# Transposing two row tiles ahead of the first modulation columns, with filler matmuls between the small steps, in a fused adaLN, linear attention and SwiGLU block

## The chip, the cores and the metric

The kernel runs on one core of one Trainium2 chip. The metric is its time in device microseconds; the span of a profile is about 2 us shorter than the time of the same execution. All times are medians, with the lowest and the highest run. There is a second number for each run, the mean clock granted to TensorE, where 1.000 is full speed; 3.4 us at half speed shows as 0.998. It counts only what the clock record lists. The record starts at 5.48 us in the profile before, and the fillers ahead of that already ran at half speed (0.43 us from start to start, 0.22 us after it). This first slow stretch is in every profile (its end, seen from the fillers, lies at 5.5 to 8.4 us) and in no mean clock; "half clock" and "full clock" below are meant after it.

## The reference

The block normalises x, scales and shifts it by columns that come from a vector c (the "modulation"), applies linear attention, and then does the same with a SwiGLU feed-forward. The change touches only the start of the first half.

```python
def reference(A_x, A_wqkv, A_wo, B_x, B_w_gate, B_w_up, B_w_down, c, w_mod):
    x = A_x                                        # 1 x 2048 x 1024, bf16
    mod = (silu(c) @ w_mod).reshape(...)           # w_mod: 1024 x 6144
    sa, ca, ga, sb, cb, gb = ...                   # six rows of 1024
    h = layernorm(x) * (1 + ca) + sa               # "wsa" holds sa's weights, "wca" ca's
    x = x + ga * linear_attention(h, A_wqkv, A_wo)
    h = layernorm(x) * (1 + cb) + sb
    return x + gb * swiglu(h, B_w_gate, B_w_up, B_w_down)
```

## The kernel before

The first q matmul needs three things: normalised and transposed rows of x, the first modulation columns, and the first q weights. All of it is loaded by one queue, in this order, and no load up to the last one shown waits for a compute engine. One part of wca, wsa or wq is 512 KB.

```python
        P.dma("c", CS8[0:NDT, :], cv8)
        for st in range(4):
            P.dma("x0_%d" % st, XRES[:, st, :], xv[:, st, :])
        # ... cut: ca_load, wq_load, sa_load issue one part each ...
        for p in range(4):
            ca_load(p)
            sa_load(p)
            if p < 3:
                wq_load(p)
        for i in range(6, 8):
            P.dma("wq%d" % i, ...)
        # then four row tiles of x for chunk 1, then the k weights
```

A filler is a matmul of a zero tile with the identity, into a bank that is overwritten before anybody reads it. It only keeps TensorE busy.

```python
        def warm(n=1, bank=2):
            for _ in range(n):
                P.pe("matmul", out=PS[:, bank, :], lhsT=IDENT[:], rhs=E1[:, 0, :], start=True, stop=True)
```

The modulation columns are products with one moving column, and 16 of them make the two columns of one pair. `fin_ca` is the small column arithmetic on VectorE; `h0_first` and `h0_scale` scale and shift the transposed rows with the columns.

```python
        def mod_pair(p):
            mod_sc(WCA, 8, range(2 * p, 2 * p + 2))
            mod_sc(WSA, 0, range(2 * p, 2 * p + 2))
            for f in fin_ca(p):
                f()
            for dt in range(2 * p, 2 * p + 2):
                h0_scale(dt)
```

The q phase of the first chunk takes the weights in parts as they land. (`mod_pair` is written out here; the kernel puts its first two lines into a helper.)

```python
            for nt in range(5):
                q_part(nt, qb[nt], (0, 1), 0, 256)      # first half of the rows
            tile_transposes(2)
            tile_transposes(3)
            # ... cut: scaling and copies of the second half ...
            for nt in range(5):
                if nt == 3:
                    mod_pair(1)
                q_part(nt, qb[nt], (0, 1), 256, 512)
            # ... cut: nt 5 and 6 ...
            for nt in range(7):
                if nt == 4:
                    mod_pair(2)
                q_part(nt, qb[nt], (2, 3))
            for nt in range(7):
                if nt == 4:
                    mod_pair(3)                         # needs the last wca and wsa parts
                q_part(nt, qb[nt], (4, 5))
            # ... cut: dt 6 and 7, and the eighth group; then k, and all the rest
```

Of the kernel before, what the change touches and what calls it, by code (L numbers as in the profile page):

```python
# [264 lines left out]
def bass_adaLN_cond__linear_attn_block__swiglu_ffn__prompt_kernel(  # L265
# [22 lines left out]
    with ExitStack() as es:  # L288
# [6 lines left out]
        def T(name, off, shape, dt):  # L295
            n = 1
            for s_ in shape[1:]:
                n *= s_
            assert off % 32 == 0 and off + n * mybir.dt.size(dt) <= ARENA, (name, off, shape)
            return nc.alloc_sbuf_tensor_at(name, shape, dt, offset=base + off)  # L300
# [4 lines left out]
        WCA = T("wca", 32 * KB, [128, NDT, D], BF16)  # L305
# [134 lines left out]
# [3 lines that stand above are left out]
# [23 lines left out]
        def ln1_xn(st):  # L466
            P.dve("tensor_scalar", out=XRES[:, st, :], in0=XRES[:, st, :],
                  scalar1=MV[:, st, 0:1], scalar2=RSTD[:, st:st + 1], op0=ALU.subtract, op1=ALU.mult)
# [22 lines left out]
        def mod_sc(w, c0, ms):  # L491
            for m in ms:
                for kt in range(NDT):
                    P.pe("matmul", out=PS[:, 0, c0 + m:c0 + m + 1], lhsT=w[:, kt, m * 128:(m + 1) * 128],
                         rhs=SILUC[:, kt:kt + 1], start=mod_first[0], stop=(kt == NDT - 1), skip_group_check=True)
                    mod_first[0] = False

        def fin_ca(p):
            sl, sp = slice(2 * p, 2 * p + 2), slice(8 + 2 * p, 10 + 2 * p)
            return [  # L500
                lambda: P.dve("tensor_copy", out=MODTMP[:, sp], in_=PS[:, 0, sp]),
                lambda: P.dve("tensor_copy", out=MODTMP[:, sl], in_=PS[:, 0, sl]),
                lambda: P.dve("tensor_scalar", out=MODTMP[:, sp], in0=MODTMP[:, sp], scalar1=1.0, scalar2=None,
                              op0=ALU.add),
                lambda: P.dve("tensor_copy", out=MODCOL[:, 1, sl], in_=MODTMP[:, sl]),
                lambda: P.dve("tensor_copy", out=MODCOL[:, 0, sl], in_=MODTMP[:, sp]),
            ]
# [12 lines left out]
        def t_view(dt, n=1):  # L520
            return PSB[:, 6 + dt // 4, (dt % 4) * 256:(dt % 4 + n) * 256]

        def h0_first(dt, half, eng):
            dst = HT[:, 0, dt, 256 * half:256 * half + 256]
            if eng == "act":
                P.act("activation", out=dst, in_=t_view(dt), func=ACT.Identity, scale=MODCOL[:, 0, dt:dt + 1],
                      bias=MODCOL[:, 1, dt:dt + 1])
            else:
                P.dve("tensor_scalar", out=dst, in0=t_view(dt), scalar1=MODCOL[:, 0, dt:dt + 1],
                      scalar2=MODCOL[:, 1, dt:dt + 1], op0=ALU.mult, op1=ALU.add)  # L530

        def raw_copy(dt, n, half, eng):
            dst = HT[:, 1, dt:dt + n, 256 * half:256 * half + 256]
            src = t_view(dt, n).rearrange("p (d q) -> p d q", q=256)
            if eng == "act":
                P.act("activation", out=dst, in_=src, func=ACT.Copy)
            else:
                P.dve("tensor_copy", out=dst, in_=src)
# [5 lines left out]
        def ln1_rstd1(st):  # L544
            P.dve("tensor_scalar", out=VE[:, st:st + 1], in0=MV[:, st, 1:2], scalar1=EPS, scalar2=None, op0=ALU.add)
            P.pool("tensor_tensor", out=RSTD[:, st:st + 1], in0=VE[:, st:st + 1], in1=NEGHALF[:, 0:1], op=ALU.pow)
# [19 lines left out]
        def act_mv_ops(st):  # L566
            return [
                lambda: P.dve("tensor_copy", out=MV[:, st, 0:1], in_=SUMX[:, st:st + 1]),
                lambda: P.dve("scalar_tensor_tensor", out=MV[:, st, 1:2], in0=SUMX[:, st:st + 1],
                              scalar=SUMX[:, st:st + 1], in1=SUMSQ[:, st:st + 1], op0=ALU.mult, op1=ALU.subtract),  # L570
            ]

        def neg_rstd(st):
            P.dve("tensor_scalar", out=VE[:, st:st + 1], in0=MV[:, st, 1:2], scalar1=-1.0, scalar2=EPS, op0=ALU.mult,
                  op1=ALU.add)
            P.pool("tensor_tensor", out=RSTD[:, st:st + 1], in0=VE[:, st:st + 1], in1=NEGHALF[:, 0:1], op=ALU.pow)

        def mixed_mv_ops(st):
            return [
                lambda: P.dve("bn_aggr", out=MV[:, st, :], in_=STATS[:, (st // 4) % 2, st % 4, 0:1, :]),  # L580
                lambda: P.dve("scalar_tensor_tensor", out=MSQ2[:, st:st + 1], in0=MV[:, st, 0:1], scalar=MV[:, st, 0:1],
                              in1=MV[:, st, 1:2], op0=ALU.mult, op1=ALU.add),
                lambda: P.dve("scalar_tensor_tensor", out=MV[:, st, 0:1], in0=MV[:, st, 0:1], scalar=0.5,
                              in1=SUMX[:, st:st + 1], op0=ALU.mult, op1=ALU.add),
                lambda: P.dve("scalar_tensor_tensor", out=SUMSQ[:, st:st + 1], in0=MSQ2[:, st:st + 1], scalar=0.5,
                              in1=SUMSQ[:, st:st + 1], op0=ALU.mult, op1=ALU.add),
                lambda: P.dve("scalar_tensor_tensor", out=MV[:, st, 1:2], in0=MV[:, st, 0:1], scalar=MV[:, st, 0:1],
                              in1=SUMSQ[:, st:st + 1], op0=ALU.mult, op1=ALU.subtract),
            ]
# [4 lines left out]
        m2, m3 = act_mv_ops(2), mixed_mv_ops(3)  # L594

        def tile_transposes(j):
            for dt in range(NDT):
                c = (dt % 4) * 256 + (j % 2) * 128
                P.pe("transpose", out=PSB[:, 6 + dt // 4, c:c + 128], in_=XRES[:, j, dt * 128:(dt + 1) * 128],
                     identity=IDENT[:])  # L600

        warm(11, bank=3)
        mod_sc(WCA, 8, range(2))
        warm(3, bank=3)
        fa = fin_ca(0)
        s0_[0]()
        s0_[1]()
        s1_[0]()
# [2 lines left out]
        s1_[1]()  # L611
        ln1_xn(0)
        tile_transposes(0)
        s1_[2]()
        ln1_rstd1(1)
        s3_[0]()
        m2[1]()
        m2[0]()
        m3[0]()
        neg_rstd(2)  # L620
        fa[0]()
        ln1_xn(1)
        fa[2]()
        m3[1]()
        fa[4]()
        m3[2]()
        mod_sc(WSA, 0, range(2))
        tile_transposes(1)
        m3[3]()
        m3[4]()  # L630
        fa[1]()
        neg_rstd(3)
        fa[3]()
        h0_first(0, 0, "dve")
        h0_first(1, 0, "dve")
        raw_copy(4, 4, 0, "act")
        raw_copy(2, 2, 0, "dve")
        ln1_xn(2)
        ln1_xn(3)

        phi_ctr = [0]
# [521 lines left out]
```

## Time and profile before

| | before |
|---|---|
| time, median of 3 runs | 840.45 us (840.42 to 840.97) |
| span of the profiled run | 838.5 us |
| TensorE busy | 98% of the span |
| first q matmul starts | 13.59 us |
| last shift columns (wsa, pair 3) start | 26.52 us |
| half clock, after the first rise at 5.48 us | 8.89 to 15.72 us |

Three lines of the page of the kernel before: the span, busy time by engine with its share, and the chain of waits by engine.

```profile
span 838.5 us, 10210 instructions
...
PE 825.3 (98%) x4154; PEld 384.1 (46%) x4233; DVE 298.3 (36%) x641; ACT 203.8 (24%) x355; POOL 41.0 (5%) x52
...
PE 95%; SPq 2%; DMA 1%; DVE 1%; issue 1%; ACT 0%; DVEq 0%
...
```

A busy TensorE says nothing of what starts it. The chain of waits of the kernel before, cut to the head, has start, length, and what ran or was waited for (SPq is the sync engine's queue, that is, the issuing of a load):

```profile
17.38 0.47 SPq L178
...
17.89 8.58 DMA wsa<-in_w_mod_dram
26.48 0.04 issue
26.52 2.84 PE ps L178 x26
...
```

Up to 26.48 us the chain is loads and the issuing of loads. From 26.52 us on it is nearly all TensorE. So the span is the start of the last shift columns plus what follows; here 838.5 - 26.52 = 812.0 us. This "rest" is used throughout.

TensorE in the head, in order of time: start, length, operation, tiles, shapes, count, and in brackets the idle time before it and what ended that. "e_92,ident" are fillers, "ident,xres" transposes, "siluc,wca" and "siluc,wsa" modulation columns, "ht,wqk" q matmuls.

```profile
2.76 3.87 PE L178 MATMUL ps<-e_92,ident 128*128 128x512 bf16 x11 [0.37 <-DVE e_92 L178]
9.38 0.59 PE L178 MATMUL ps<-siluc,wca 128*128 128x1 bf16 x16 [2.75 <-DMA wca<-in_w_mod_dram]
...
11.06 1.06 PE L178 MATMUL ps<-ident,xres 128*128 128x128 bf16 x8
...
12.39 1.01 PE L178 MATMUL ps<-ident,xres 128*128 128x128 bf16 x8
13.59 2.29 PE L178 MATMUL ps<-ht,wqk 128*128 128x256 bf16 x10 [0.19 <-DVE ht L178]
...
22.30 0.54 PE L178 MATMUL ps<-siluc,wsa 128*128 128x1 bf16 x16
...
26.52 0.55 PE L178 MATMUL ps<-siluc,wsa 128*128 128x1 bf16 x16 [0.18 <-DMA wsa<-in_w_mod_dram]
...
```

The fillers end at 6.63 us, and TensorE idles 2.75 us until the first wca part has landed. Then everything follows in a row, the two transposes among it. TensorE waited only 0.18 us for the last wsa part.

Stages of the kernel before: the stretch and its length, busy time by engine (PE is TensorE, PEld its weight loads, DVE VectorE, ACT ScalarE, POOL GpSimd; x counts instructions), then the granted clock, the DMA engines' share and their rate.

```profile
core 0: us, PE busy (x) PEld busy (x) DVE busy (x) ACT busy (x) POOL busy (x), PEclk, DMA share, GB/s
...
6.00:10.00 4.00, 1.25 (x20) 0.66 (x19) 2.62 (x11) 3.50 (x7) 1.67 (x3) 0.86 1.10 316
10.00:14.00 4.00, 3.81 (x37) 2.61 (x36) 2.63 (x14) 0.81 (x3) 0.55 (x1) 0.50 1.15 318
...
22.00:26.00 4.00, 3.88 (x54) 2.18 (x54) 1.31 (x7) 0.00 (x0) 0.00 (x0) 1.00 1.12 307
...
```

From 6 us on the DMA engines' share is above 1, at 307 to 318 GB/s in these lines. (The Trainium skill, page "DMA: Bandwidth & Descriptors", section "Specifications", gives about 358 GB/s as the HBM limit for a core; these three lines are 11 to 14% below that.) The clock column shows the half clock.

### The profile page before, as it was taken

To read this page: it belongs to the slowest core of one execution; us is meant where nothing else is said; L and a number is where in the kernel's file an instruction comes from. 1 tells how busy PE (TensorE), PEld (TensorE's weight loads), DVE (VectorE), ACT (ScalarE), POOL (GpSimd) and SP (SyncE) were. 2 spreads that over 40 slices of the span, in tenths; PEclk is the share of its full clock that TensorE was granted. 3 is DMA by queue.
4 is the path that set the end of the run, shared out by engine and by line. 5 is a ranking of instruction groups with operands and counts; after the bars stand their busy time and mean duration, and the time that the engine had idled before them with its cause. 6 is when DMAs were issued, how large, how long until landed. Compare 5 with 4: busy or idle time off the path is not lost.

```text
span 838.5 us, 10210 instructions
## 1 busy us (share of the span) xinstructions
PE 825.3 (98%) x4154; PEld 384.1 (46%) x4233; DVE 298.3 (36%) x641; ACT 203.8 (24%) x355; POOL 41.0 (5%) x52
## 2 busy tenths in 40 slices
PE   7999999999999999999999999999999999999998
PEld 4444444454444444444444444444444444444444
DVE  5777966556974212111221111022121102111111
ACT  4667763213333111100111111021111101111111
POOL 1000000000050000030000003000000300000000
PEclk8999999999999999999999999999999999999999
DMA  9993323747195895540355562045556104553000
GB/s 276 265 323 48 68 89 126 172 136 265 37 248 184 266 296 155 153 80 26 108 153 153 151 157 58 24 114 151 151 150 181 46 13 113 151 152 99 1 25 26
DMA packets 178125, 112.99 MB, mean 135 GB/s; under 512 B 32664, under 2 KB 161824, under 8 KB 178080
## 3 DMA queue, kind: packets, MB, share of 16 engines
q1 hardware_dynamic: 178080, 112.35, 48.1%
q8 instruction: 33, 0.54, 0.3%
q14 instruction: 12, 0.10, 0.0%
HBM read 100.67 MB, written 4.33 MB: 125 GB/s over the span
## 4 chain that ended last, share of the span: by engine, by line
PE 95%; SPq 2%; DMA 1%; DVE 1%; issue 1%; ACT 0%; DVEq 0%
PE ps L178 95%; SPq L178 2%; DMA wsa<-in_w_mod_dram 1%; DVE acc L178 0%; DVE xres L178 0%; DVE mhl L178 0%; ACT mw L178 0%; DVE ve_72 L178 0%; DVE ut L178 0%; DVE mean_70 L178 0%; DVE msq_71 L178 0%; DVE sumx L178 0%; DVEq L249 0%
## 5 line engine op out<-in xcount | busy, mean ns | idle before, releaser
L178 DVE TENSOR_TENSOR at<-sg,ps 128x512 bf16<-128x512 bf16 x112 | 77.0, 688 | 296.1 <-PE ps L178 285.1
L178 ACT ACTIVATE sg<-ps 128x512 bf16<-128x512 f32 x112 | 66.9, 597 | 310.3 <-PE ps L178 298.9
L178 PE MATMUL ps<-wd_a,at 128*128 128x512 bf16 (+2 forms) x519 | 112.8, 372 | 0.5
L178 PE MATMUL ps<-wd_b,at 128*128 128x512 bf16 (+2 forms) x388 | 85.4, 372 | 0.5
L178 PEld LDWEIGHTS ps<-wd_a,at 128*128 128x128 bf16 x528 | 51.1, 98 | 59.8
L178 DVE TENSOR_TENSOR ut<-att,gb_b 128x512 bf16<-128x512 bf16 (+1 forms) x32 | 13.5, 421 | 167.7 <-ACT att L178 167.7
L178 ACT ACTIVATE att<-ps 128x512 bf16<-128x512 f32 (+1 forms) x32 | 17.4, 591 | 182.1 <-PE ps L178 182.1
L178 PE MATMUL ps<-ht,wqk 128*128 128x512 bf16 (+1 forms) x258 | 58.4, 376 | 1.0 <-DVE ht L178 0.5
L178 PEld LDWEIGHTS ps<-wd_b,at 128*128 128x128 bf16 x396 | 38.3, 98 | 44.7
L178 PE MATMUL ps<-wqk,ht 128*128 128x512 bf16 x250 | 56.6, 379 | 0.4
L178 PE MATMUL ps<-mw,pqt 128*128 128x512 bf16 x250 | 55.8, 379 | 0.4
L178 PE MATMUL ps<-h2t,guu_117 128*128 128x512 bf16 x221 | 52.8, 379 | 0.2
L178 PE MATMUL ps<-h2t,guu_115 128*128 128x512 bf16 x219 | 52.6, 379 | 0.3
L178 PE MATMUL ps<-h2t,gug_114 128*128 128x512 bf16 x220 | 52.6, 379 | 0.2
L178 PE MATMUL ps<-h2t,guu_116 128*128 128x512 bf16 x221 | 52.6, 379 | 0.2
L178 PE MATMUL ps<-h2t,gug_111 128*128 128x512 bf16 x220 | 52.5, 379 | 0.2
L178 PE MATMUL ps<-h2t,gug_112 128*128 128x512 bf16 x219 | 52.5, 379 | 0.2
L178 PE MATMUL ps<-h2t,gug_113 128*128 128x512 bf16 x219 | 52.3, 379 | 0.3
L178 PE MATMUL ps<-h2t,guu_118 128*128 128x512 bf16 x217 | 52.1, 379 | 0.3
L178 POOL TENSOR_SCALAR h2t<-h2t,modcol 128x512 bf16<-128x512 bf16 x32 | 28.3, 898 | 394.4 <-DMA h2t<-xn_119 394.4
L178 ACT ACTIVATE e_92<-ps 128x512 bf16<-128x512 f32 x64 | 39.1, 611 | 30.8 <-PE ps L178 27.0
L178 ACT ACTIVATE rl<-ps 128x512 bf16<-128x512 f32 x64 | 38.9, 608 | 0.0
(120 smaller groups left out, 685.5 us busy)
## 6 DMA issues: line engine op xcount, KB each, us to landing
gug_111<-in_B_w_gate_dram SPq DMA_DIRECT2D x14, 512.0 KB, 4.0
guu_115<-in_B_w_up_dram SPq DMA_DIRECT2D x14, 512.0 KB, 5.3
gug_112<-in_B_w_gate_dram SPq DMA_DIRECT2D x14, 512.0 KB, 4.0
guu_116<-in_B_w_up_dram SPq DMA_DIRECT2D x14, 512.0 KB, 5.3
gug_113<-in_B_w_gate_dram SPq DMA_DIRECT2D x14, 512.0 KB, 4.0
guu_117<-in_B_w_up_dram SPq DMA_DIRECT2D x14, 512.0 KB, 5.3
gug_114<-in_B_w_gate_dram SPq DMA_DIRECT2D x14, 512.0 KB, 4.1
guu_118<-in_B_w_up_dram SPq DMA_DIRECT2D x14, 512.0 KB, 5.3
```

The source lines that it names most:

```text
L178: return getattr(e, method)(**kw)
```

## The change

Its intent is to take the wait for the first wca part out of TensorE's path: the transposes of tiles 0 and 1 need no modulation, so they can fill it; tile 1 is normalised earlier for that. The fillers are there to keep the clock at full speed. 14 fillers are removed and 22 added. In the diff, `ln1_xn(j)` normalises row tile j, the `s_`, `m2`, `m3` and `neg_rstd` calls are steps of the rows' statistics, `fa` those of `fin_ca(0)`, and `raw_copy` saves transposed rows for a later pair:

```diff
-        warm(11, bank=3)
-        mod_sc(WCA, 8, range(2))
-        warm(3, bank=3)
         fa = fin_ca(0)
+        warm(13, bank=3)
         # ... cut: statistics and normalisation of tile 0 ...
         tile_transposes(0)
+        warm(2, bank=3)
         s1_[2]()
         ln1_rstd1(1)
         s3_[0]()
+        ln1_xn(1)
+        tile_transposes(1)
+        warm(0, bank=3)
+        mod_sc(WCA, 8, range(2))
+        warm(4, bank=3)
         # ... cut: m2, m3[0], neg_rstd(2) ...
+        m3[1]()
+        m3[2]()
         fa[0]()
-        ln1_xn(1)
+        ln1_xn(2)
         fa[2]()
-        m3[1]()
+        m3[3]()
         fa[4]()
-        m3[2]()
+        m3[4]()
         mod_sc(WSA, 0, range(2))
-        tile_transposes(1)
-        m3[3]()
-        m3[4]()
+        warm(3, bank=3)
+        neg_rstd(3)
         fa[1]()
-        neg_rstd(3)
+        raw_copy(4, 4, 0, "act")
         fa[3]()
         h0_first(0, 0, "dve")
         h0_first(1, 0, "dve")
-        raw_copy(4, 4, 0, "act")
         raw_copy(2, 2, 0, "dve")
-        ln1_xn(2)
         ln1_xn(3)
```

## The prediction

> **What bounds the kernel now.** The page gives TensorE 98% of an 838.5 us span. The change touches only the first 14 us: does a gain there reach the end? In the chain of waits, nothing of the first 26.5 us is TensorE: it is the sync engine issuing loads ([...]2.97 us for the first 512 KB of q weights), then 8.58 us of the last shift-modulation load (wsa part 3). From 26.52 on it is nearly all TensorE, back to back. The stage table shows the DMA engines saturated (share about 1.0 or more, about 320 GB/s) from 4 to 33 us.
>
> Landings, from each issue's start plus its time to landing: wca part 0 9.4, wsa 0 11.0, wq 0 12.5, wca 1 14.3, wsa 1 16.0, wq 1 17.5, wca 2 19.8, wsa 2 21.5, wq 2 23.1, wca 3 24.9, wsa 3 26.5 us. None waits for a compute engine.
>
> **What TensorE does in the head.** Fillers end at 6.6; it idles 2.75 us until wca 0 lands. The granted clock falls to 0.50 at 8.9 and returns at 15.7. The Trainium skill ("TensorE: Matmul & The Clock Gate", Part 1) says free-running windows of 3413 ns set the clock; the trace agrees: the stretches last 3.41 us (full) and 6.83 us (half). Row tile 0, normalised at 7.5, is transposed only at 10.6, tile 1 at 12.4; the first q matmul starts at 13.6.
>
> **What the change does.** Removes 11+3 fillers, adds 13+2+4+3 (net +8, an estimated 0.22 us each at full clock, 1.7 us, in gaps). Both tiles' transposes (1.0 us each at half clock, about 0.5 at full) move ahead of the modulation columns; tile 1's normalisation (0.55 us on VectorE) moves from 10.1 to about 8.5. Estimates: fillers to 7.1, tile 0 transposed 7.6 to 8.1, tile 1 9.1 to 9.6, wca columns to 10.1, fillers to 11.0, wsa columns to 11.6, column arithmetic and scaling of h on VectorE, first q matmul 12.5 to 12.8 (wq 0 lands 12.5). The clock stays full through 16 us, or drops for one window.
>
> **What of it is on the critical path.** TensorE comes to the second half-tile q work 1 to 2 us earlier, but then meets loads: wsa 1 (16.0), wsa 2 (21.5; before it used them at 22.3, so at most 0.8 us is left), wsa 3 (26.5; before it used them at 26.52 after waiting 0.18 us). There nothing is left; the saved time turns into waits for loads. Load order and later stages are unchanged.
>
> **Time.** 840.4 us, range 839.7 to 841.1. Faster by over 2% would need 16.8 us.
>
> **What would show it.** First q matmul at 12.5 to 12.8 (not 13.6). No half clock between 9 and 16 us, or one window. TensorE's waits for wca and wsa loads between 14 and 27 us growing from 0.2 to 1 to 2.5 us. Wsa 3 columns still at 26.5 us, within 0.3; first k matmul (33.1) unmoved; the chain of waits still with loads to 26.5.
>
> **What would make it wrong.** Loads landing earlier because the engines compete less with them (a gain to about 1 us). New idling before wsa 2 and wsa 3 falling badly into a clock window and halving the clock around 27 us (a loss of about 3 us). Fillers or the new VectorE order delaying the first q matmul by more than 1 to 2 us of slack.

## The result, and the profile after

The changed kernel took 839.93 us (839.89 to 841.08, 4 runs), the kernel before 840.43 us (840.24 to 840.97, 4 runs). The ratio is 0.9996, with a 95% interval of 0.9979 to 1.0014: the same. Ratios are the mean time of one kernel's fast runs over that of the other's of the same rounds, so not quite the ratio of the medians quoted.

The same lines of the changed kernel's page:

```profile
span 837.9 us, 10302 instructions
...
PE 829.9 (99%) x4241; PEld 383.6 (46%) x4241; DVE 299.7 (36%) x641; ACT 203.8 (24%) x355; POOL 40.9 (5%) x52
...
PE 96%; SPq 2%; DMA 1%; DVE 1%; issue 0%; ACT 0%; DVEq 0%
...
```

The PE counts must not be compared: 87 more matmuls are listed where the change adds 8 fillers (the weight loads, PEld, differ by just 8), so 79 matmul records are missing in the trace before.

TensorE in the head of the changed kernel (columns as before):

```profile
2.76 4.75 PE L178 MATMUL ps<-e_92,ident 128*128 128x512 bf16 x13 [0.36 <-DVE e_92 L178]
7.68 0.62 PE L178 MATMUL ps<-ident,xres 128*128 128x128 bf16 x8 [0.17 <-DVE xres L178]
...
9.21 0.62 PE L178 MATMUL ps<-ident,xres 128*128 128x128 bf16 x8 [0.47 <-DVE xres L178]
9.66 0.54 PE L178 MATMUL ps<-siluc,wca 128*128 128x1 bf16 x16
...
12.46 1.39 PE L178 MATMUL ps<-ht,wqk 128*128 128x256 bf16 x10 [0.33 <-DVE ht L178]
...
20.83 0.55 PE L178 MATMUL ps<-siluc,wsa 128*128 128x1 bf16 x16 [0.42 <-DMA wsa<-in_w_mod_dram]
...
25.85 0.55 PE L178 MATMUL ps<-siluc,wsa 128*128 128x1 bf16 x16 [0.96 <-DMA wsa<-in_w_mod_dram]
...
```

Both transposes now precede the wca columns, the 2.75 us wait is gone, and the first q matmul starts at 12.46 us, 1.13 us earlier. But then TensorE waits 0.42 us for wsa part 2 and 0.96 us for wsa part 3, where before it waited 0.18 us in all. Its gain has become two waits.

The chain of waits of the changed kernel:

```profile
17.15 8.65 DMA wsa<-in_w_mod_dram
25.80 0.05 issue
25.85 34.26 PE ps L178 x214
```

It has the same shape. The rest is 837.9 - 25.85 = 812.05 us, against 811.98 us before. So all of the 0.6 us by which this span is shorter is that one load landed at 25.80 us, not at 26.48 us. Whether the change caused that is a question for the experiments.

Stages of the changed kernel:

```profile
6.00:10.00 4.00, 3.36 (x38) 1.80 (x37) 3.46 (x15) 3.84 (x9) 1.58 (x3) 1.00 1.14 323
10.00:14.00 4.00, 3.67 (x48) 2.35 (x45) 3.02 (x13) 0.89 (x1) 0.65 (x2) 1.00 1.16 310
...
22.00:26.00 4.00, 3.04 (x34) 1.50 (x32) 0.74 (x2) 0.00 (x0) 0.00 (x0) 1.00 1.14 329
...
```

The clock is full in all these stages (in the first from 6.39 us on), and the DMA rate is the same within a few per cent.

### The profile page after: what moved, and what is told of

Read it like the earlier page. It is cut to its first block, busy times and chain, and to the rows that moved or that the text cites. A ratio compares the mean times of both kernels' runs of the same rounds, so it can differ in the third digit from the quotient of the medians.

```text
span 837.9 us, 10302 instructions
## 1 busy us (share of the span) xinstructions
PE 829.9 (99%) x4241; PEld 383.6 (46%) x4241; DVE 299.7 (36%) x641; ACT 203.8 (24%) x355; POOL 40.9 (5%) x52
## 4 chain that ended last, share of the span: by engine, by line
PE 96%; SPq 2%; DMA 1%; DVE 1%; issue 0%; ACT 0%; DVEq 0%
PE ps L178 96%; SPq L178 2%; DMA wsa<-in_w_mod_dram 1%; DVE acc L178 0%; DVE xres L178 0%; DVE mhl L178 0%; ACT mw L178 0%; DVE ve_72 L178 0%; DVE ut L178 0%; DVE mean_70 L178 0%; DVE msq_71 L178 0%; DVE sumx L178 0%; DVEq L249 0%
```

## The experiments

Theory A: the loads set the head; what the change saves on TensorE turns into waits for the later modulation loads, and the rest, 812.0 us, is untouched. Rival B: TensorE's own work and clock bound the head, and the 0.5 us between the medians is the change's gain. Rival C: the change saves nothing that would last even without those loads. Every run is marked as correct, e7 and e8 too, where the results are wrong, so for these two the mark says nothing. Each was timed in five rounds, beside the kernel before; an interval is about 1 us to either side, so a difference below that is read from the profiles.

A summary of one profiled execution of each, in us. "Last columns" is the start of the last shift columns, and the rest is the span minus that.

| run | time (lowest to highest) | before, same rounds | first q | last columns | rest |
|---|---|---|---|---|---|
| before, first profile | 840.43 (840.24 to 840.97) | - | 13.59 | 26.52 | 811.98 |
| changed, first profile | 839.93 (839.89 to 841.08) | 840.43 | 12.46 | 25.85 | 812.05 |
| r_before | 840.51 (840.05 to 840.73) | 840.47 | 12.68 | 26.59 | 812.01 |
| r_after | 840.72 (839.87 to 841.07) | 840.47 | 12.59 | 26.69 | 812.01 |
| e1_order_only | 840.59 (840.01 to 840.82) | 840.47 | 12.21 | 26.20 | 812.00 |
| e2_fill_only | 840.21 (840.05 to 840.46) | 840.47 | 13.54 | 26.19 | 812.01 |
| e3_delay4 | 840.57 (840.20 to 842.22) | 840.52 | 12.47 | 26.09 | 812.01 |
| e4_delay14 | 842.73 (841.62 to 844.40) | 840.52 | 12.31 | 28.71 | 811.99 |
| e5_extra_load | 842.82 (842.01 to 845.46) | 840.52 | 12.87 | 28.51 | 814.89 |
| e6_q7_early | 840.39 (839.76 to 842.51) | 840.52 | 12.27 | 27.05 | 811.25 |
| e7_light_before | 839.05 (837.63 to 840.04) | 840.75 | 12.86 | 24.98 | 812.02 |
| e8_light_after | 838.09 (837.95 to 838.39) | 840.75 | 12.30 | 23.94 | 811.96 |
| e9_q7_mid | 840.27 (839.98 to 840.52) | 840.75 | 12.62 | 26.11 | 811.89 |
| e10_load_fill | 842.39 (841.97 to 844.12) | 840.65 | 12.36 | 30.04 | 812.06 |

### r_before and r_after: both kernels again

No edit.

> The kernel before, again, as a control. Both theories: ratio 1.000 within 0.1%. Its use is the spread of the landing of the last shift-modulation load (26.5 us in the first profile) and of the clock record in the head: if the landing moves by some 0.5 us from execution to execution of one program, the 0.68 us by which it was earlier in the changed kernel's profile is no work of the change.

> The changed kernel again. Theory A (the loads set the head, the change only turns TensorE work into waits): ratio to before 1.000 within 0.1%; the last shift-modulation load lands where it lands in the control, within 0.3 us. Rival B (full clock and earlier work are worth the 0.5 us that the medians show): 0.4 to 0.7 us faster than before, again, and the load lands 0.5 us or more earlier than in the control.

Measured: 840.51 us and 840.72 us, against 840.47 us for the runs of before (ratios 0.9999, 0.9986 to 1.0011, and 1.0001, 0.9988 to 1.0013). TensorE in the head of r_before, and then of r_after:

```profile
12.68 1.71 PE L178 MATMUL ps<-ht,wqk 128*128 128x256 bf16 x10 [0.19 <-DVE ht L178]
...
26.59 0.55 PE L178 MATMUL ps<-siluc,wsa 128*128 128x1 bf16 x16 [0.74 <-DMA wsa<-in_w_mod_dram]
...
```

```profile
12.59 1.39 PE L178 MATMUL ps<-ht,wqk 128*128 128x256 bf16 x10 [0.32 <-DVE ht L178]
...
26.69 0.55 PE L178 MATMUL ps<-siluc,wsa 128*128 128x1 bf16 x16 [0.90 <-DMA wsa<-in_w_mod_dram]
...
```

The 0.5 us of the first comparison is gone: this time the changed kernel's last columns started later than the control's (26.69 and 26.59 us). The landing of the last load moves by 0.8 us between two executions of one program (25.85 and 26.69 us for the changed kernel), and the span moves with it. The kernel before also shows it in its own head: its first q matmul came at 13.59 us in one execution and at 12.68 us in the other. In the second the first wca columns started 0.26 us earlier, with their load, and the half clock began later (10.19 to 13.60 us, not 8.89 to 15.72), so that these columns and the fillers after them still ran at full clock. These 0.9 us moved the last columns by 0.07 us. Against this control the changed kernel's first q matmul (12.59 us) is only 0.09 us earlier: most of the 1.13 us of the first pair was the draw of the old order. What makes the landing vary was not studied, but part of it is there from the first wca part on, which landed at 8.5 us in the first profile of the changed kernel and at 9.3 us in r_after.

Rival B's first support has fallen. Of the prediction's checks, "within 0.3 us of 26.5" holds for these two, not for the first profile of the changed kernel (25.85).

### e1_order_only: the changed order with the first 11 fillers alone

```diff
-        warm(13, bank=3)
+        warm(11, bank=3)
-        warm(2, bank=3)
-        warm(0, bank=3)
-        warm(4, bank=3)
-        warm(3, bank=3)
```

> The changed order, but with the first 11 fillers alone. Theory A: the clock halves for some 7 us from about 9 us, the first q matmul comes at 12.5 to 14 us, the last shift-modulation columns still start at their load's landing, and the time is that of the changed kernel within 0.4 us. Rival B: slower than the changed kernel by 0.5 us or more, back to before's time.

Measured: 840.59 us, ratio 1.0000 (0.9986 to 1.0014). The clock did halve, but only from 13.11 to 16.52 us, after the first q matmul, which started at 12.21 us. So the clock part of the expectation missed in place and length, and the first q matmul came 0.3 us ahead of the range expected; the time and the rest (812.00 us) are as theory A has them. All five runs had a mean clock below 1 (0.996 to 0.998), and it cost nothing that can be seen against before.

### e2_fill_only: the old order with more fillers

```diff
-        warm(11, bank=3)
+        warm(24, bank=3)
         mod_sc(WCA, 8, range(2))
```

> The old order, with 24 instead of 11 fillers, so that TensorE does not idle before the first modulation columns. Theory A: no half clock, the first q matmul 0.5 to 1 us earlier than in the kernel before (about 12.6 to 13.1 us), and the time of both other kernels within 0.4 us. Rival B: 0.4 us or more faster than before, if the clock is what pays.

Measured: 840.21 us, ratio 0.9996 (0.9984 to 1.0009); the mean clock was 1.000 in all five runs (the first slow stretch, here to 7.85 us, is not in it). TensorE in its head:

```profile
10.44 0.54 PE L178 MATMUL ps<-siluc,wca 128*128 128x1 bf16 x16
...
13.54 1.39 PE L178 MATMUL ps<-ht,wqk 128*128 128x256 bf16 x10 [0.59 <-DVE ht L178]
...
```

The first q matmul came at 13.54 us, not at 12.6 to 13.1: the fillers, of which 12 started before the clock rose at 7.85 us, held TensorE until the wca columns could start only at 10.44 us. That expectation missed. But it makes the point better: with a full clock and with a first q matmul as late as in the later profile of before, the time is the same, and the last columns start at 26.19 us. Neither the clock nor the first q matmul decides.

### e3_delay4 and e4_delay14: fillers put where TensorE waited

Bank 0's unused columns take the fillers, with zeros added.

```diff
                 if nt == 4:
+                    for _ in range(4):          # 14 in e4_delay14
+                        P.pe("matmul", out=PS[:, 0, 16:512], lhsT=IDENT[:], rhs=E1[:, 0, 0:496],
+                             start=False, stop=True, skip_group_check=True)
                     mod_pair(3)
```

> The changed kernel with 4 fillers (0.21 us each, 0.84 us in all) ahead of the last modulation columns, where TensorE waited 0.96 and 0.90 us in its two profiles. Theory A: the wait shrinks to 0 to 0.3 us, the last shift-modulation columns still start when their load lands (25.8 to 26.7 us), the rest of the span after that start stays 812.0 us, and the time is within 0.1% of before and after. Rival B (TensorE's own work bounds the head): 0.8 us slower than the changed kernel.

> The same with 14 fillers, 2.9 us. Theory A: the first 1.0 us is free, the rest is not: 1.5 to 2.2 us slower (a median of 842.0 to 842.7), no wait for the load left, the rest of the span after the start of the last shift-modulation columns still 812.0 us. Rival B: the whole 2.9 us slower.

Measured: with 4 fillers 840.57 us, ratio 1.0003 (0.9991 to 1.0015). TensorE around the last columns of e3_delay4:

```profile
24.64 1.00 PE L178 MATMUL ps<-e,ident 128*128 128x496 bf16 x4
...
26.09 0.55 PE L178 MATMUL ps<-siluc,wsa 128*128 128x1 bf16 x16
...
```

The profile still shows a wait of 0.72 us at wsa part 2 and lists none for part 3; the rest is 812.01 us. The times alone do not tell a cost of 0.8 us from none, as the interval is about 1 us to either side. The profile does: the fillers lie in the former wait, and the chain of waits has the last wsa load landing at 26.05 us, so the last columns, at 26.09 us, were still released by their load. So 0.84 us of work there is free. With 14 fillers 842.73 us, ratio 1.0025 (1.0012 to 1.0038): the median is 2.2 us above before's of the same rounds, so some 0.7 us of 2.9 were free, a little less than expected (the kernel before stands in for the changed one, which was not timed in these rounds). TensorE around the last columns of e4_delay14:

```profile
25.37 3.09 PE L178 MATMUL ps<-e,ident 128*128 128x496 bf16 x14
...
28.71 0.54 PE L178 MATMUL ps<-siluc,wsa 128*128 128x1 bf16 x16
...
```

No wait is left at these columns, and the rest is 811.99 us. Both fit theory A. Rival B, for which all 2.9 us would have been paid, does not fit the 2.2 us, though by a margin that the interval (1.0 to 3.2 us) does not quite carry alone. The traces settle it: the last wsa load of this execution landed at 26.4 us; without the fillers TensorE would have come to its columns at 25.8 us (an estimate: 25.37 plus 0.4 us of wca columns) and waited some 0.7 us. The constant rest does not tell A from B; it only says that nothing after the last columns changed. The part that is free is less than the 0.96 us of the first profile: in this execution wsa part 2 came late, and TensorE reached the place of the fillers at 25.37 us, not at 24.34.

### e5_extra_load: one more load ahead of the last two

```diff
         for p in range(4):
+            if p == 3:
+                P.dma("extra", STG[:, :, 0:256], wmv[:, :, 2048:2304])
             ca_load(p)
             sa_load(p)
```

> The changed kernel with one more load of 512 KB, whose data nobody reads, ahead of the last two modulation loads. Theory A: at the head's 300 to 330 GB/s it takes about 1.6 to 1.75 us, so the last shift-modulation columns start 1.4 to 2.0 us later (27.5 to 28.4 us), TensorE waits 2.3 to 2.9 us for them, and the time grows by 1.4 to 2.0 us (841.9 to 842.5). Rival B: less than 0.8 us slower.

Measured: 842.82 us, ratio 1.0033 (1.0021 to 1.0044), 2.3 us over before's median. One load of 512 KB is paid for in full, and more: the expectation was 1.4 to 2.0 us. The one run at a mean clock of 1.000 took 842.01 us, inside it; the three at 0.998 took 842.18 to 843.00 us, the two at 0.996 844.66 and 845.46 us, and one of these two was profiled. TensorE around the last columns there, and then three stretches of that execution cut at the changes of the clock (columns as in the stage tables above; the third is left out):

```profile
26.73 0.55 PE L178 MATMUL ps<-siluc,wca 128*128 128x1 bf16 x16 [1.55 <-DMA wca<-in_w_mod_dram]
28.51 0.59 PE L178 MATMUL ps<-siluc,wsa 128*128 128x1 bf16 x16 [1.23 <-DMA wsa<-in_w_mod_dram]
...
```

```profile
core 0: us, PE busy (x) PEld busy (x) DVE busy (x) ACT busy (x) POOL busy (x), PEclk, DMA share, GB/s
24.57:27.98 3.41, 1.17 (x19) 0.56 (x17) 0.00 (x0) 0.00 (x0) 0.00 (x0) 1.00 1.15 324
27.98:31.39 3.41, 2.88 (x22) 1.31 (x23) 1.51 (x8) 0.86 (x1) 0.00 (x0) 0.50 1.06 379
...
```

TensorE waited 1.55 and 1.23 us, so it was busy for only 1.17 of the 3.41 us up to 27.98, and the clock was half for the next 6.83 us. The rest grew from 812.0 to 814.89 us. This is what the prediction feared under "new idling before wsa 2 and wsa 3", and with a longer wait it is real.

### e6_q7_early: matmuls moved into the wait

```diff
             for nt in range(7):
-                if nt == 4:
-                    mod_pair(3)
                 q_part(nt, qb[nt], (4, 5))
+            mod_pair(3)
+            q_part(7, 0, range(6))
         # ... cut ...
-            q_part(7, 0, range(NDT))
+            q_part(7, 0, (6, 7))
```

> An attempt to use the wait: the six q matmuls that stood behind the last modulation columns go ahead of them (into the wait), and six of the eighth q group's matmuls go behind them, to cover the time in which VectorE scales h. The work after the load that lands last shrinks by 6 matmuls (1.3 us). Theory A: TensorE reaches the columns 0.3 us late or just in time, idles 0.4 to 0.7 us for VectorE, and the time falls by 0.3 to 0.8 us (839.6 to 840.2); the rest of the span after the start of the last shift-modulation columns falls from 812.0 to about 811.2 us. Rival B: no change of that rest, as the order of work does not alter its sum.

Measured: 840.39 us, ratio 1.0001 (0.9989 to 1.0013). TensorE there:

```profile
22.69 4.12 PE L178 MATMUL ps<-ht,wqk 128*128 128x512 bf16 x17
...
27.05 0.54 PE L178 MATMUL ps<-siluc,wsa 128*128 128x1 bf16 x16
27.98 4.92 PE L178 MATMUL ps<-ht,wqk 128*128 128x512 bf16 x21 [0.38 <-DVE modtmp L178]
...
```

The rest fell to 811.25 us as expected, with 0.38 us of idling for VectorE. But the time did not fall: TensorE came to the last columns only at 27.05 us. In this execution wsa part 2 landed late (its columns started at 21.84 us), and with six matmuls more between the two there was no slack to make that good. The gain is the size of the loads' own variation. The time part of the expectation, and its 0.3 to 0.8 us, was not shown.

### e7_light_before and e8_light_after: the later modulation loads left out

Both kernels give wrong results. In both, the loads of parts 1 to 3 of wca and wsa are left out, and part 0 is used for all columns. Every instruction of the compute engines stays.

```diff
         for p in range(4):
-            ca_load(p)
-            sa_load(p)
+            if p == 0:
+                ca_load(p)
+                sa_load(p)
         # ... cut ...
-                    ... lhsT=w[:, kt, m * 128:(m + 1) * 128], ...
+                    ... lhsT=w[:, kt, (m % 2) * 128:(m % 2 + 1) * 128], ...
```

> Wrong results on purpose. The kernel before, with modulation loads 1 to 3 (3 MB) left out, and the columns of all pairs computed from load 0; all the work of the engines stays. Now the q weights land from 12.5 us on, one part per 1.7 us, faster than TensorE uses them, so TensorE's own work bounds the head. Both theories: 3 to 6 us faster than before (834.5 to 837.5). To be set against the next.

> Wrong results on purpose. The changed kernel with the same loads left out. Theory A (the change's gain at the first q matmul is real, and the late modulation loads swallow it): with those loads gone it comes through: 0.7 to 2.0 us faster than the kernel before with the same loads left out, spread by where the clock window falls in the old order. Rival C (the change gains nothing that lasts, loads or no loads): equal within 0.3 us.

Measured: the old order took 839.05 us (837.63 to 840.04), the new 838.09 us (837.95 to 838.39); their ratios to the full kernel before are 0.9979 (0.9965 to 0.9993) and 0.9969 (0.9956 to 0.9981). TensorE in the head of the old order, then of the new, without those loads:

```profile
12.86 1.87 PE L178 MATMUL ps<-ht,wqk 128*128 128x256 bf16 x10 [0.19 <-DVE ht L178]
...
24.98 0.54 PE L178 MATMUL ps<-siluc,wsa 128*128 128x1 bf16 x16
...
```

```profile
12.30 1.39 PE L178 MATMUL ps<-ht,wqk 128*128 128x256 bf16 x10 [0.33 <-DVE ht L178]
...
23.94 0.54 PE L178 MATMUL ps<-siluc,wsa 128*128 128x1 bf16 x16
...
```

In neither does TensorE wait for a modulation load after part 0. In the profiled pair all of the difference at the last columns, 1.04 us, reaches the end: the spans are 837.0 and 835.9 us, the rests 812.02 and 811.96 us. The medians differ by 0.96 us, inside the 0.7 to 2.0 us of theory A, and over rival C's 0.3 us. In the chain of waits the old order's head is still released by a load, the first wca part, up to 9.39 us, while the new order's goes back to the first rows of x and their normalisation, and to no modulation load. But the first wca part landed at 9.4 us in the old order's profile and at 8.6 us in the new one's, so part of the 1.04 us can be that draw. And the intervals of the two ratios overlap, and so do the two sets of five runs: the fastest run of the old order (837.63 us, mean clock 1.000) beats all runs of the new, and one at 839.98 us, also at 1.000, is not explained. What can be said is that the new order's runs lie within 0.44 us and the old order's within 2.41 us, and that the profiled old order had a half clock from 10.70 to 14.11 us, which the new one has not.

The first of the two missed its own size: leaving 3 MB out gained 1.7 us, not 3 to 6. Theory A bounds the full kernels by loads, but by no more than that; TensorE's own work follows closely behind.

### e9_q7_mid: a milder form of the attempt

The edit of e6_q7_early, but with the last modulation pair ahead of the seventh group, so that two matmuls stay behind it.

```diff
             for nt in range(7):
-                if nt == 4:
+                if nt == 6:
                     mod_pair(3)
                 q_part(nt, qb[nt], (4, 5))
+            q_part(7, 0, range(6))
         # ... cut ...
-            q_part(7, 0, range(NDT))
+            q_part(7, 0, (6, 7))
```

> A milder form of the attempt with the eighth q group: only four of the six matmuls go ahead of the last modulation columns, two stay behind, and six of the eighth group's follow. Theory A: TensorE reaches the columns 0.43 us earlier than in that attempt, about when the load lands; the rest of the span after their start is 811.3 us (within 0.15), and the time 839.6 to 840.3, at most 0.7 us below the changed kernel, which five rounds hardly resolve.

Measured: 840.27 us, ratio 0.9994 (0.9982 to 1.0007): the lowest ratio of the correct kernels, and not resolved from 1. The rest was 811.89 us, not 811.3. TensorE:

```profile
26.11 0.55 PE L178 MATMUL ps<-siluc,wsa 128*128 128x1 bf16 x16 [0.16 <-DMA wsa<-in_w_mod_dram]
...
33.45 8.81 PE L178 MATMUL ps<-wqk,ht 128*128 128x512 bf16 x39 [0.47 <-DMA wqk<-in_A_wqkv_dram]
```

The k matmuls now start earlier, and wait 0.47 us for the second half of their first weights: the next load in the line takes the bound over. As it stands the attempt pays nothing that can be shown.

### e10_load_fill: the extra load, with the waits filled

The kernel of e5_extra_load, with 6 fillers ahead of the last scale columns and 5 between them and the shift columns.

```diff
         def mod_pair(p):
-            mv_pair(p)
+            if p == 3:
+                fill0(6)                        # the fillers of e3_delay4
+                mod_sc(WCA, 8, range(6, 8))
+                fill0(5)
+                mod_sc(WSA, 0, range(6, 8))
+            else:
+                mv_pair(p)
```

> The kernel with the extra load again, with 6 fillers ahead of the last scale-modulation columns and 5 between them and the shift columns (2.3 us of fillers, in the 1.55 and 1.23 us for which TensorE waited there). Its clock record fell to 0.50 from 28.0 to 34.8 us in the profiled run, and in five of six runs the mean clock was below 1.0. Theory A with the clock as its second part (idling for late loads halves the clock in the next window, and that alone made the runs of the extra load spread from 842.0 to 845.5): with the waits filled the mean clock is 1.0 in at least four of five runs, all of those lie at 841.9 to 842.8, the rest of the span after the start of the last shift columns is 812.0 us (it was 814.89), and the median falls by 0 to 0.6 us. Rival D (the spread is of the load's own landing): the spread stays above 2 us whatever the clock.

Measured: 842.39 us, ratio 1.0020 (1.0006 to 1.0034). Four of five runs had a mean clock of 1.000, at 841.97, 841.99, 842.39 and 842.67 us, as expected; without fillers it was one of six. The fifth, at 844.12 us and 0.998, is the profiled one: there TensorE waited 0.54 and 1.22 us for the pair before, where there are no fillers, and the clock was half from 23.60 to 27.01 us. The rest is 812.06 us. So the spread of e5_extra_load came mostly from the clock, against rival D, and fillers in a wait protect what comes after it. (E10 ran on another chip than the other experiments; the kernel before had 1.000 in one of nine runs there and in two of nine or eleven in the other rounds, so that chip does not favour a full clock.) They do not shorten the wait, and they can overrun it: in the profiled run TensorE, slowed by that half clock, came to the fillers at 27.34 us and to the last columns at 30.04 us, while their load had landed at 28.4 us.

## Why the prediction was right

- **The time.** 840.4 us was predicted, in 839.7 to 841.1; measured 839.93, and 840.72 in the second set of rounds. Right.
- **The start.** First q matmul at 12.5 to 12.8 us: 12.46 and 12.59 us. No half clock between 9 and 16 us: right in both profiles of the changed kernel. But "not 13.6" was one draw of the old order: against the control, at 12.68 us, the first q matmul gains only 0.09 us.
- **The waits.** They were to grow from 0.2 to 1 to 2.5 us: 0.18 us before, 0.42 + 0.96 = 1.38 us and 1.19 + 0.90 = 2.09 us after. But 0.2 us was one execution's value: the control of the kernel before waits 0.86 + 0.74 = 1.60 us, as it came to these columns earlier, its half clock being later and shorter. Against it the waits grew by 0.49 us, not by 1.20. The prediction took a single profile for the kernel.
- **Nothing is left at 26.52 us.** The rest is 811.98 to 812.06 us in the nine profiled executions that keep the order of q matmuls after the last columns and full clock there (of both kernels, r_before, r_after, e1 to e4 and e10), whatever the first q matmul (12.21 to 13.59 us) and whether the clock fell earlier. That alone would hold under rival B too; what tells them apart is that e5 shows that a later load is paid, and e3 that 0.84 us of work ahead of the load is not.
- **What failed.** "Wsa 3 columns still at 26.5 us, within 0.3; first k matmul (33.1) unmoved": in the first profile after they were at 25.85 and 32.41 us. The loads' landing itself was taken as fixed, and it moves by 0.8 us between executions of one program. It moved the result by as much as any other term. With the change it does not visibly move: the last wsa part landed at 26.2 to 26.6 us in the three profiles of the old order with all its loads, and at 25.8 to 26.7 us in the seven of the new order without the extra load. A shift of some 0.2 us would not be seen in so few, so the prediction's "loads landing earlier" is not ruled out at that size. That the time came out so near the middle of the range is in part luck of these draws.
- **The feared clock loss.** Two of nine runs of the changed kernel have a mean clock of 0.998 and took 841.07 and 841.08 us, the slowest of their sets; so are the runs at 0.998 of e3, e4 and e6 (842.22, 844.40 and 842.51 us). That fits a half clock after the new waits, as e5 shows it; none of these was profiled, so where it fell stays open.

## What to carry to other kernels

Before speeding up the start of a busy engine, follow the chain of waits to the first point from which that engine never waits again; what lies ahead of that point is worth only the wait that is left there. Check such a point over several executions, since loads and clock windows move by a microsecond and one profile shows one draw. A cheap test is to put idle work into the wait: if it costs nothing, making the work before it faster gains nothing either.

## What the Trainium skill lacked or had wrong

- "TensorE: Matmul & The Clock Gate", Part 1, says the half clock comes "after ≥1 idle window (~3.4µs)", and "Why this matters for your kernels" asks for gaps of no more than about 3 us. The window length agrees (3.41 us). But the clock fell here after windows that were far from idle: TensorE was busy for 1.15 of 3.41 us in the kernel before (5.48 to 8.89), 1.57 in r_before (6.77 to 10.19), 1.17 in e5 and 1.93 in e10, the longest single wait being 2.75 us; it stayed full after 1.98 us in e1 (6.28 to 9.70; after the next window there, with 1.84 us, it fell), 2.22 us in r_after (19.55 to 22.96) and 2.46 us in the changed kernel (23.45 to 26.87). The page has no busy share for this.
- The same page, Part 4, says of transposes that "HAM K=8/8 doesn't engage for transpose-mode", and gives about 275 ns for one in a kernel. Neither holds here: one took 219 ns at full clock and 314 ns at half clock in the kernel before (265 ns is only the mean over the two), and eight in a row took 0.62 us at full and 1.01 to 1.06 us at half clock. They overlap, and they do follow the granted clock.
- No page that was found says how much a landing varies between executions of one program: here the last modulation load, the 16th in a row, let its columns start at 25.85 us in one execution of the changed kernel and at 26.69 us in another.
